# Row-wise softmax units from unit 6 on, earlier modulation weights, group loads one per pair, and P buffers given out by release, in a fused attention and gMLP block

## The chip, the cores and the metric

The kernel runs on one core of one Trainium2 chip. The metric is device time in microseconds (us). On one core there is no second die to compare with, so a run counts as fast when it lies within 1.5% of the fastest run of the same kernel. "Same": within 2%. Differences of a few us are given as ratios with a 95% interval, and the places where they arise are read from the traces.

## The reference

```python
mod = (_silu(c) @ w_mod).reshape(c.shape[0], 6, 1, -1)      # sa, ca, ga, sb, cb, gb: 512 each
h = _layernorm(x) * (1 + ca) + sa                           # x: 1 x 2048 x 512
x = x + ga * _A_ref(h, k_cache, v_cache, wq, wo)            # 32 heads, 8 K/V heads, 2048 keys, Dh 128
h = _layernorm(x) * (1 + cb) + sb
x = x + gb * _B_ref(h, w_in, w_sp, b_sp, w_out)             # gMLP with a 2048 x 2048 spatial matmul
```

Everything is bf16 in and out. `_A_ref` is plain softmax attention with four query heads to each K/V head. `ga` and `gb` are row vectors that scale the outputs of the two halves; the kernel needs them as rows repeated on all 128 partitions, `ga` first when the last K/V group's results are added, `gb` in the last matmul of the gMLP.

## The kernel before

Attention is cut into 128 units, `u = 16 * g + j`: one K/V group `g` (8 of them) and one tile `j` of 128 queries, with the group's four heads. Iteration `it` of the main loop holds unit `it`'s QK matmuls and exponentials, in 8 slots; into the same slots go the PV matmuls of an earlier unit, the output projection (Wo) of a still earlier one, and the Q projection of a later chunk. A unit comes in one of two forms.

* By columns: QK gives scores with keys on the partitions, ScalarE writes P already transposed (`pT`), PV takes 64 matmuls of 129 columns, and its small result `onorm` (128 x 512) goes through one DMA transpose to `oT`.
* By rows: QK gives scores with queries on the partitions, ScalarE writes P into four row buffers `pn` (three in the later home of `w_in`, called `win_sb`, one in `wmod_a`), VectorE scales it, and four DMA transposes of 128 x 2048, one per head, make `pT`. PV then takes 16 matmuls of 512 columns.

```python
TURN_A, TURN_B = 3 * CT, (HKV - 1) * NT            # 12, 112
def by_rows(u):
    return TURN_A <= u < TURN_B and u % 2 == 0
def pv_at(u):
    return u + 3 if by_rows(u) else u + 1
...
def turn_rows(u, hh):                              # two slots after the head's exponentials
    ...                                            # VectorE: sum, reciprocal, scale pn[hh]
    nc.sync.dma_start_transpose(out=pTs[u][:, :, hh * P : (hh + 1) * P], in_=pn[hh])
...
def mod_rows():                                    # ga and gb as rows
    mc_ps = bank("misc")
    for i, row in enumerate((0, 3)):
        mod_part(i, wmod_b, row * D, mc_ps)        # 16 matmuls of one column each
    for i, (part, rows) in enumerate(((2, ga_rows), (5, gb_rows))):
        cols = slice(part * NDT, (part + 1) * NDT)
        nc.vector.tensor_copy(out=modc[:, cols], in_=mc_ps[:, i * NDT : (i + 1) * NDT])
        line = dram.tile([D], FP32, name=f"mod{part}")
        nc.gpsimd.dma_start(out=line[:].rearrange("(dt p) -> p dt", p=P), in_=modc[:, cols])
        nc.gpsimd.dma_start(out=rows[:], in_=line[:].partition_broadcast(P))
...
at(2, 5, lambda: nc.gpsimd.dma_start(out=wmod_b, in_=wmod_dram[:, :, 2 * D : NMOD]))   # 2 MB
at(9, 4, mod_cols_b)
at(10, 4, mod_rows)
```

`at(it, slot, fn)` puts work into a slot. The last two lines of `mod_rows` are a round trip through DRAM: 512 floats are written, which turns a column layout into a line, and read back broadcast to all partitions. There are two such trips, one for `ga` and one for `gb`, both on GpSimd's queue, one behind the other. In this text they are called the trips.

## Time and profile before

| | before |
|---|---|
| median of three runs | 1317.13 us (1315.36 to 1318.52) |
| span of the profiled run, mean granted clock | 1314.1 us, 0.999 |
| row units | 50: units 12, 14, ... 110 |
| TensorE, ideal stream | 1293.1 us |
| TensorE, idle | 14.0 us |

The last two rows are worked out as in the prediction below, which also names the source of the time that a matmul is given: what a matmul takes over that time, from its start to the next one's, is counted as idle. It can be summed unit by unit.

The page's busy times and its DMA queues (packets, MB, share of 16 engines' time):

```profile
PE 1305.1 (99%) x9959; PEld 755.5 (57%) x9959; DVE 657.4 (50%) x1612; ACT 1105.0 (84%) x1461; POOL 52.0 (4%) x96
...
q1 hardware_dynamic: 530592, 135.97, 60.3%
```

The list of TensorE's waits (who waits, line, for whom: us in total, times, longest):

```profile
PE s_ps L1013 <- ACT wmod_a L1001: 1.6, 1, 1.6
PE o_ps L785 <- DVE onorm L767: 1.2, 1, 1.2
PE s_ps L1013 <- ACT pT L1020: 0.2, 1, 0.2
```

TensorE is busy 99% of the span, and no wait in the list is over 2 us. The first is the one late transpose of a row unit that the prediction finds at 541 us. GpSimd's timeline shows where the trips stood:

```profile
104.96 0.76 POOL L1173 DMA_DIRECT2D mod<-modc  x1 [42.79 <-DVE modc L1171]
113.98 0.56 POOL L1174 DMA_DIRECT2D ga_rows<-mod  x1 [8.27 <-DMA mod<-modc]
114.53 0.76 POOL L1173 DMA_DIRECT2D mod<-modc  x1
126.35 0.55 POOL L1174 DMA_DIRECT2D gb_rows<-mod  x1 [11.05 <-DMA mod<-modc]
```

The first trip was over before the first transposes of row unit 12 (121.4 us). Only the end of the second met them. The first two landed 8.5 and 11.2 us after their issue (the median of their form is 4.9), but TensorE did not wait for them. The loads of K/V group 2 were long done by then (59 to 61 us).

### The profile page before, as it was taken

To read this page: it belongs to the slowest core of one execution; us is meant where nothing else is said; L and a number is where in the kernel's file an instruction comes from. 1 tells how busy PE (TensorE), PEld (TensorE's weight loads), DVE (VectorE), ACT (ScalarE), POOL (GpSimd) and SP (SyncE) were. 2 spreads that over 40 slices of the span, in tenths; PEclk is the share of its full clock that TensorE was granted. 3 is DMA by queue.
4 is the path that set the end of the run, shared out by engine and by line. 5 is a ranking of instruction groups with operands and counts; after the bars stand their busy time and mean duration, and the time that the engine had idled before them with its cause. 6 is when DMAs were issued, how large, how long until landed. Compare 5 with 4: busy or idle time off the path is not lost.

```text
span 1314.1 us, 25092 instructions
## 1 busy us (share of the span) xinstructions
PE 1305.1 (99%) x9959; PEld 755.5 (57%) x9959; DVE 657.4 (50%) x1612; ACT 1105.0 (84%) x1461; POOL 52.0 (4%) x96
## 2 busy tenths in 40 slices
PE   9999999999999999999999999999999999999998
PEld 5666555555555555555555555555556666644445
DVE  6624445444454544444455544444452566784444
ACT  7899999999999999999999999999998899650000
POOL 1101000000000000000000000000000000120000
PEclk9999999999999999999999999999999999999999
DMA  7554988878988888988897877688762232143200
GB/s 181 123 67 58 180 161 141 140 125 158 153 144 138 144 141 138 135 142 157 153 143 129 155 141 144 124 166 151 140 126 76 45 62 48 29 117 80 69 21 27
DMA packets 537741, 156.79 MB, mean 119 GB/s; under 512 B 527280, under 2 KB 533680, under 8 KB 537616
## 3 DMA queue, kind: packets, MB, share of 16 engines
q1 hardware_dynamic: 530592, 135.97, 60.3%
q0 software_dynamic: 4432, 16.91, 4.6%
q10 hardware_dynamic: 2592, 2.23, 0.5%
q8 instruction: 80, 1.31, 0.4%
q14 instruction: 45, 0.37, 0.1%
HBM read 21.89 MB, written 2.10 MB: 18 GB/s over the span
## 4 chain that ended last, share of the span: by engine, by line
PE 98%; DMA 1%; DVE 0%; issue 0%; ACT 0%; ACTq 0%; DVEq 0%
PE o_ps L1069 21%; PE s_ps L1013 20%; PE o_ps L1048 13%; PE s_ps L994 13%; PE misc L1101 8%; PE misc L944 8%; PE misc L1426 7%; PE s_ps L1260 2%; PE s_ps L1299 2%; PE o_ps L1447 1%; DMA pT<-wmod_a 1%; PE o_ps L785 1%; PE s_ps L1447 1%; PE misc L854 0%; PE o_ps L944 0%; DVE hT L813 0%
## 5 line engine op out<-in xcount | busy, mean ns | idle before, releaser
L1020 ACT ACTIVATE wsp<-s_ps 128x1024 bf16<-128x1024 f32 x408 | 416.2, 1025 | 19.5 <-PE s_ps L1013 3.5
L1013 PE MATMUL s_ps<-qT,kT 128*128 128x512 bf16 x1248 | 370.9, 379 | 1.9 <-ACT wmod_a L1001 1.6
L1001 ACT ACTIVATE win_sb<-s_ps 128x1024 bf16<-128x1024 f32 x300 | 307.0, 1025 | 6.2 <-ACT win_sb L1001 0.8
L1069 PEld LDWEIGHTS <-wsp 128*128 128x128 bf16 x3264 | 218.5, 98 | 96.3
L1069 PE MATMUL o_ps<-v,wsp 128*128 128x129 bf16 x3264 | 251.6, 220 | 0.0
L994 PE MATMUL s_ps<-kT,qT 128*128 128x512 bf16 x800 | 237.9, 379 | 0.0
L1048 PE MATMUL o_ps<-pT,v 128*128 128x512 bf16 x800 | 237.3, 379 | 0.0
L1020 ACT ACTIVATE pT<-s_ps 128x1024 bf16<-128x1024 f32 x216 | 217.3, 1026 | 20.6 <-PE s_ps L1013 8.3
L1101 PE MATMUL misc<-wo_g,oT 128*128 128x512 bf16 x512 | 194.0, 379 | 0.0
L1013 PEld LDWEIGHTS <-kT 128*128 128x128 bf16 x1248 | 121.0, 98 | 117.0 <-issue 4.4
L944 PE MATMUL misc<-hT,wq_g 128*128 128x512 bf16 (+2 forms) x520 | 187.0, 371 | 0.1
L1069 PEld LDWEIGHTS <-pT 128*128 128x128 bf16 x1728 | 115.3, 98 | 49.6
L955 DVE CAST qT<-misc 128x512 bf16<-128x512 f32 x125 | 85.5, 684 | 112.2 <-PE misc L944 112.2
L1048 PEld LDWEIGHTS <-v 128*128 128x128 bf16 x800 | 78.2, 98 | 94.4
L1069 PE MATMUL o_ps<-v,pT 128*128 128x129 bf16 x1728 | 132.5, 220 | 0.0
L1057 DVE CAST oT<-o_ps 128x512 bf16<-128x512 f32 x50 | 34.6, 691 | 173.7 <-PE o_ps L1048 173.7
L1035 DVE TENSOR_SCALAR win_sb<-win_sb,rall 128x2048 bf16<-128x2048 bf16 x150 | 113.0, 753 | 5.7 <-DVE rall L1034 0.5
L994 PEld LDWEIGHTS <-qT 128*128 128x128 bf16 x800 | 78.2, 98 | 52.5 <-issue 0.2
L1001 ACT ACTIVATE wmod_a<-s_ps 128x1024 bf16<-128x1024 f32 x100 | 102.4, 1024 | 2.3 <-DMA pT<-wmod_a 2.3
L1426 PE MATMUL misc<-wsp,z 128*128 128x512 bf16 (+2 forms) x560 | 100.7, 336 | 0.0
L1080 DVE RECIPROCAL rall<-o_ps 128x2 f32<-128x2 f32 x156 | 26.6, 170 | 135.1 <-PE o_ps L1069 131.4
L1031 DVE TENSOR_TENSOR tot<-rs 128x1 f32<-128x1 f32 x200 | 30.7, 154 | 120.6 <-ACT win_sb L1001 119.1
(106 smaller groups left out, 856.5 us busy)
## 6 DMA issues: line engine op xcount, KB each, us to landing
wq_g<-in_A_wq_dram POOLq DMA_DIRECT2D x7, 512.0 KB, 5.5
v<-in_A_v_cache_dram POOLq DMA_DIRECT2D x7, 512.0 KB, 5.9
wo_g<-in_A_wo_dram POOLq DMA_DIRECT2D x7, 512.0 KB, 3.8
pT<-win_sb SPq DMA_TRANSPOSE x150, 4.9
wsp<-in_w_mod_dram POOLq DMA_DIRECT2D x1, 2048.0 KB, 10.4
out_dram<-yout ACTq DMA_DIRECT2D x16, 128.0 KB, 1.7
win_sb<-in_B_w_in_dram POOLq DMA_DIRECT2D x1, 1792.0 KB, 9.3
x_sb<-in_A_x_dram SPq DMA_DIRECT2D x3, 512.0 KB, 5.3
```

The costliest lines, as they stand in the source:

```text
L944: nc.tensor.matmul(ps[0][:, o0 : o0 + n], lhsT=wqs[g][:, dt, hh * DH : (hh + 1) * DH], rhs=hTs[ch][:, dt, c0 : c0 + n], start=(dt == 0), s ...
L955: nc.vector.tensor_copy(out=dst, in_=src)
L994: nc.tensor.matmul(s_ps[:, c * 512 : (c + 1) * 512], lhsT=qTs[b][:, hh, jj * P : (jj + 1) * P], rhs=groups[g]["kT"][:, k0 : k0 + 512], sta ...
L1001: nc.scalar.activation(out=pn[hh][:, half * HK : (half + 1) * HK], in_=s_ps[:], func=ACT.Exp, scale=inv_sqrt_dh, accum_out=rsums[u][:, i : ...
L1013: nc.tensor.matmul(s_ps[:, h * 512 : (h + 1) * 512].rearrange("p (r q) -> p r q", r=REP), lhsT=groups[g]["kT"][:, kt * P : (kt + 1) * P], ...
L1020: nc.scalar.activation(out=pTs[u][:, 2 * i : 2 * i + 2, :], in_=s_ps[:].rearrange("p (k q) -> p k q", k=2), func=ACT.Exp, scale=inv_sqrt_dh,)
L1035: nc.vector.tensor_scalar(out=pn[hh], in0=pn[hh], scalar1=rinv, scalar2=None, op0=ALU.mult)
L1048: nc.tensor.matmul(o_pss[u][:], lhsT=groups[g]["v1"][:, kt, 0:DH], rhs=pTs[u][:, kt, :], start=(kt == 0), stop=(kt == NKT - 1),)
L1057: nc.vector.tensor_copy(out=oTs[u][:], in_=o_pss[u][:].rearrange("p (r q) -> p r q", r=REP))
L1069: nc.tensor.matmul(o_ps[:, hh % 2, 0 : DH + 1], lhsT=pTs[u][:, kt, hh * P : (hh + 1) * P], rhs=groups[g]["v1"][:, kt, 0 : DH + 1], start=( ...
L1101: nc.tensor.matmul(X_ps[:], lhsT=oTs[u][:, hh, :], rhs=groups[g]["wo"][:, hh, :], start=(hh == 0), stop=(hh == REP - 1),)
L1426: nc.tensor.matmul(g_ps[:, :n], lhsT=z2[:, st, f * P : (f + 1) * P], rhs=wsp[t][:, st, c0 : c0 + n], start=(st == 0), stop=(st == NT - 1 a ...
```

## The change

Its intent: take more units in the form by rows, which costs TensorE a little less, by beginning with them at unit 6 rather than 12 and by adding units 112, 116 and 120; to have what they need in time, load the modulation weights earlier and compute their columns and rows in iterations 4 and 5 (the big buffer `wsp` that holds the weights then serves as a P buffer); spread each group's Wq, K, V and Wo loads over one load per pair of units; and give three P buffers out by whichever is released first.

```diff
-    TURN_A, TURN_B = 3 * CT, (HKV - 1) * NT
+    TURN_A, TURN_B = CT + 2, (HKV - 1) * NT
     def by_rows(u):
-        return TURN_A <= u < TURN_B and u % 2 == 0
+        return u % 2 == 0 if TURN_A <= u < TURN_B else u % 4 == 0 and TURN_B <= u < NU - CT
     def pv_at(u):
-        return u + 3 if by_rows(u) else u + 1
+        return u + 1 if not by_rows(u) else u + 3 if u < TURN_B else u + 5
+    users, homes = dict(pT0=-2, pT1=-1, wsp=TURN_A), {}
+    for u in range(NU):
+        homes[u] = min(users, key=lambda k: users[k])
+        assert users[homes[u]] < u
+        users[homes[u]] = pv_at(u)
...
-    at(2, 5, lambda: nc.gpsimd.dma_start(out=wmod_b, in_=wmod_dram[:, :, 2 * D : NMOD]))
-    at(TURN_B + 3, 5, lambda: nc.gpsimd.dma_start(out=win_sb, in_=win_dram))
-    at(9, 4, mod_cols_b)
-    at(10, 4, mod_rows)
+    at(2, 1, lambda: nc.gpsimd.dma_start(out=wmod_b, in_=wmod_dram[:, :, 2 * D : NMOD]))
+    at(NU - CT - 1, 2, lambda: nc.gpsimd.dma_start(out=win_sb, in_=win_dram))
+    at(4, 4, mod_cols_b)
+    at(5, 4, mod_rows)
...
-    at(TURN_B + 4, 0, wsp0)
+    at(NU + 1, 0, wsp0)
     for st in range(NT):
-        at(TURN_B + 4 + st // 2, 2 + 4 * (st % 2), lambda st=st: load_wsp(wsp[0], 0, st))
+        at(NU + 1 + st // 4, 2 * (st % 4), lambda st=st: load_wsp(wsp[0], 0, st))
     for g in range(1, HKV):
         it = (g - 1) * NT
-        at(it + 7, 6, lambda g=g: load_k(g))
-        at(it + 8, 3, lambda g=g: load_v(g))
-        at(it + 9, 3, lambda g=g: load_wo(g, nc.gpsimd))
-        at(it + 7, 3, lambda g=g: load_wq(g, nc.gpsimd))
+        at(it + 7, 4, lambda g=g: load_wq(g, nc.gpsimd))
+        at(it + 9, 5, lambda g=g: load_k(g))
+        at(it + 11, 4, lambda g=g: load_v(g))
+        at(it + 13, 4, lambda g=g: load_wo(g, nc.gpsimd))
```

Cut away here: the choice of tile in `qk`, the slots of the Q projection, and the lists of PV and Wo units in the main loop, which follow from the above.

More of the change, by code (lines that the diff above doesn't have):

```diff
@@ L982, in qk @@
         if i == 0:
-            if TURN_A <= u <= TURN_B + 1 and u % 2 == 1:
+            if homes[u] == "wsp":
                 pTs[u] = wspp.tile([P, NT, 512], BF16, name="wsp")
             else:
-                pTs[u] = late.tile([P, NKT, 512], BF16, name="pT")
+                pTs[u] = late.tile([P, NKT, 512], BF16, name=homes[u], bufs=1)
             if by_rows(u):
@@ L1230, in set_fill @@
             if hole:
-                it, slot = hole, k // 2
+                it, slot = divmod(hole * NSLOT + k // 2 - 1, NSLOT)
             if b == 1:
                 it, slot = 2 + (10 + k) // 16, (5 + k // 2) % 8
-            elif b == 2:
-                it, slot = (5, k // 2) if k < 8 else (it, slot)
             fill.setdefault((it, slot), []).append(fn)
@@ L1350 @@
             zs["z2"] = z2p.tile([P, NT, FH], BF16, name="z2")
-        pvs = [u for u in (it - 3, it - 1) if 0 <= u < NU and pv_at(u) == it]
-        wos = [u for u in (it - 5, it - 3) if 0 <= u < NU and pv_at(u) + 2 == it]
+        pvs = [u for u in (it - 5, it - 3, it - 1) if 0 <= u < NU and pv_at(u) == it]
+        wos = [u for u in (it - 7, it - 5, it - 3) if 0 <= u < NU and pv_at(u) + 2 == it]
         wf = [fn for u in wos for fn in wo_proj(u)]
```

## The prediction

> **What bounds the kernel now.** I read the page first, then the chain that ended last in order of time, then the timelines of single engines. The page's chain, by engine:
>
> ```profile
> PE 98%; DMA 1%; DVE 0%; issue 0%; ACT 0%; ACTq 0%; DVEq 0%
> ```
>
> TensorE is the bound almost everywhere, so the question is how dense its stream is. The same chain in order of time (start, length, piece) gives its rate:
>
> ```profile
> 72.35 0.45 PE o_ps L1069 x8
> ...
> 528.82 13.25 DMA pT<-wmod_a
> ...
> 1154.81 12.09 PE s_ps L1299 x56
> ```
>
> 56 matmuls of 512 columns in 12.09 us are 216 ns each; 8 of 129 columns in 0.45 us are 56 ns each. The DMA piece is the one large wait in the attention part: the fourth transpose of one row unit landed 13.25 us after its issue (the median of that form is 4.3), and PE lost 1.8 us (start-to-start distances of the matmuls, less 216 or 56 ns each).
>
> A unit by columns is 16 QK matmuls of 512, 64 PV matmuls of 129, and on average 4 of Wo and 4 of the Q projection: 24 x 0.2158 + 64 x 0.0563 = 8.78 us. A unit by rows replaces the 64 by 16 of 512: 40 x 0.2158 = 8.63 us. ScalarE's timeline shows both (start, length, instruction):
>
> ```profile
> 59.18 35.15 ACT L1020 ACTIVATE pT<-s_ps 128x1024 bf16<-128x1024 f32 x32 [0.29 <-PE s_ps L1013]
> ...
> 158.58 8.52 ACT L1020 ACTIVATE wsp<-s_ps 128x1024 bf16<-128x1024 f32 x8
> ...
> 176.02 8.52 ACT L1020 ACTIVATE wsp<-s_ps 128x1024 bf16<-128x1024 f32 x8
> ```
>
> Columns alone: (35.15 - 1.02)/31 x 8 = 8.81 us a unit. A pair of one row and one column unit: 176.02 - 158.58 = 17.44 us, which leaves 8.63 for the row unit. So turning a column unit into a row unit is worth only 0.17 us to PE. ScalarE is close behind: from 149.76 to 219.52 us, four pairs, it is busy 68.02 of 69.76 us.
>
> Subtracting the ideal stream from all of PE's start-to-start distances leaves 14.0 us of idle in the run: 5.1 in the first 20 us, 1.2 in units 12 to 15 (the turn to rows, bound by ScalarE), 1.8 at the late transpose, 1.9 in the MLP, the rest grains. This is all that a better schedule can win.
>
> **What the Trainium skill says.** "TensorE: Matmul & The Clock Gate", section "Back-to-back issue gap", gives an isolated gap of N/2.4 + 2.5 ns: 215.8 for 512 columns and 56.3 for 129. The trace agrees (216 and 56); the page's "sustained" figures of 81 and 131 ns are not what this stream shows. The same page, section "Architectural detail", says VectorE and GpSimd are strict FIFO; the trace agrees for GpSimd below. "Trainium Kernel Development and Optimization", section "Key Constraints", says that DMAs of the Sync, Scalar and GpSimd queues run on the same 16 engines and interleave; the next views show what that costs.
>
> **The change part by part.**
>
> *Row units.* Before, units 12, 14, ... 110: 50. After, 6, 8, ... 110 and 112, 116, 120: 56. Six more at 0.17 us: -1.0 us.
>
> *The turn.* In units 12 to 15 PE's work is 7.92 + 7.77 + 7.92 + 6.91 = 30.5 us (one PV is missing because a row unit's PV comes three units later, and the 16 Q matmuls fill in), but ScalarE needs 31.7 (first activation at 118.03, of unit 16 at 149.76). After, units 6 to 9 hold 8.35 + 7.34 + 8.78 + 7.77 = 32.2 us, because the projection for unit 12 on is no longer taken from them. Only the first pair (15.7 against some 16.1 for ScalarE) should wait: about 0.4 us instead of 1.2, so -0.8 us.
>
> *The last group.* A PV that was doubled up in iteration 113 is now doubled in 125; both are PE bound, 0. The first 16 W_sp transposes go from 1030-1098 us to after unit 127 (about 1139 us). One takes 1.26 us to issue and 2.6 to land, so 16 take some 20 us, and the spatial matmuls that read them start at 1184.9: hidden. Loading w_in after unit 120 (some 1075-1091 us, 9.3 us to land, needed at 1130.9): hidden.
>
> *"Loads one per pair".* GpSimd's timeline shows that placement in the program does not set when its loads go:
>
> ```profile
> 249.87 0.75 POOL L720 DMA_DIRECT2D wq_g<-in_A_wq_dram  x1 [64.68 <-PE misc L944]
> ...
> 528.90 0.75 POOL L720 DMA_DIRECT2D wq_g<-in_A_wq_dram  x1 [64.68 <-PE misc L944]
> ```
>
> The load issued at 249.87 (the third of this timeline after the first group's) stands in the program at iteration 39, about 353 us; GpSimd has nothing else to do, runs ahead and issues as soon as the last projection that reads the old buffer is over. Wq, V and Wo keep their order and their releasers, so in steady state they go when they did. The Wq load at 528.90 beside the transpose issued at 528.82 is the collision behind the 13.25 us; I see nothing that removes it. It was one of seven, so it may or may not recur: -0.5 us as an expectation.
>
> *The modulation weights (2 MB).* They move from iteration 2 slot 5 to slot 1, which puts them ahead of the next norm on GpSimd. The same FIFO makes this a large move:
>
> ```profile
> 21.77 1.05 POOL L681 TENSOR_TENSOR rstd_ln<-ve_ln,mhalf 128x4 f32<-128x4 f32 x1
> 35.77 0.23 POOL L677 TENSOR_SCALAR ve_ln<-mv 128x4 f32<-128x4 f32 x1 [12.95 <-DVE mv L697]
> 36.09 1.04 POOL L681 TENSOR_TENSOR rstd_ln<-ve_ln,mhalf 128x4 f32<-128x4 f32 x1
> 37.09 0.95 POOL L1218 DMA_DIRECT2D wsp<-in_w_mod_dram  x1
> ```
>
> Before, the load waited behind the norm at 36.09. After, nothing stands between 22.8 us and it. There it meets the four transposes of the first full chunk of h (Sync's queue), for which VectorE already waits:
>
> ```profile
> 23.30 5.90 SPq L844 DMA_TRANSPOSE hT<-xn  x4
> ...
> 38.10 8.01 SPq L844 DMA_TRANSPOSE hT<-xn  x4
> ```
>
> ```profile
> 30.57 1.38 DVE L813 TENSOR_SCALAR hT<-hT,modc 128x512 bf16<-128x512 bf16 x4 [3.02 <-DMA hT<-xn]
> ```
>
> ```profile
> 32.12 0.59 PE L944 MATMUL misc<-hT,wq_g 128*128 128x512 bf16 x2
> ```
>
> At 23.30 the transposes were alone: the fourth was issued at 27.26 and landed 3.2 us later, 7.2 us in all. At 38.10 they ran beside the 2 MB: fourth issued at 43.13, landed 6.0 later, 11.0 in all. If the 11.0 moves to the first chunk, it lands at 34.3, VectorE's first scaled piece is ready at some 34.7, and PE's first projection matmul, at 32.12 before, waits until about 35: +2.6 to +3.1 us, say +3.0, on the path because PE takes matmuls in order. I give this 0.8: +2.4. The columns and rows computed from these weights move from iterations 9 and 10 to 4 and 5 (45 and 53 us); the load, 10.4 us long, is there by 33.
>
> *Three buffers of P by release.* By hand, each unit finds a buffer whose PV is at least one iteration back: columns share one, rows alternate between two, and in the last group a row unit holds one for five iterations while columns use two. No new wait, 0.
>
> Sum: -1.0 - 0.8 - 0.5 + 2.4 = +0.1 us.
>
> **The rivals.**
> 1. *Only the gains come through.* If the 2 MB are slow enough to start, or the transposes win their share of the engines, the first chunk is not late: 1317.1 - 2.3 = 1314.8. For it: the load goes only half a microsecond ahead of the first transpose. Against: at 37.09 it was a full microsecond ahead and the transposes still took 3.8 us more.
> 2. *The row transposes become the limit.* In the pairs the 16 DMA engines are 0.86 busy and a row unit's fourth buffer is reused some 13 us after its transpose is issued; Wq, V and Wo of the second group, before at 59-61 us, now follow the modulation rows (two round trips through DRAM of 8 and 11 us) and go together at some 80-85 us, into the transposes of unit 8. A landing of 13 us just fits; one or two misses like the one at 541 cost 2 us each: 1319 to 1321. Against: 44 of 50 row units live beside such loads with one miss.
> 3. *ScalarE takes over.* A row unit adds 8 accumulator reads of 0.19 us, mostly under the activations. Alone, ScalarE passed units 12 to 15 at 15.9 us a pair against PE's 17.44, so six more row units leave it behind PE: no change.
>
> **Range and chances.** Gains total at most 2 to 4 us and the one loss I see is 3, with another 2 to 4 possible: 1313 to 1320. The three runs of before alone span 3.2 us. Since the single collision is the only thing against the change and I may have overrated it, I set the point a little below the sum, at 1316.4. Two per cent is 26 us, twice all the idle time that PE has; nothing in the change moves that much, so 0.98 for within.
>
> **What would show it.** Right: 56 row units at 8.63 us; pairs at 17.44 from unit 10; VectorE's wait before the first scaling of h up from 3.02 to about 7 us and PE idle for some 3 us near 32; the modulation load issued near 22.8; Wq at unchanged times in steady state; PE idle in the turn under 0.6 us. Wrong: no PE idle near 32 (rival 1), new PE waits on transposes of P (rival 2), or a pair longer than 17.5 us (rival 3). A W_sp transpose that ends PE's wait near 1185 us would break the last-group step.

## The result, and the profile after

| | before | after |
|---|---|---|
| median | 1317.82 us (1315.36 to 1318.52, 4 runs) | 1331.49 us (1327.86 to 1334.19, 4 runs) |
| span of the profiled run, clock | 1314.1 us, 0.999 | 1329.4 us, 0.995 |
| TensorE, ideal stream | 1293.1 us | 1292.2 us |
| TensorE, idle | 14.0 us | 30.2 us |

The ratio is 1.0105, 95% interval 1.0077 to 1.0133: "same" by the 2% rule, but slower beyond doubt, and outside the predicted range of 1313 to 1320. Ratios here are the mean time of one kernel's fast runs over that of the other's fast runs of the same rounds, so not quite the ratio of the medians quoted. The medians here are of four runs of each kernel; the experiments bring their own runs of before.

The spans differ by 15.3 us: 16.2 us more idle, less 0.9 us of shorter stream. The page after, busy times, then the Sync and ScalarE DMA queue, then the chain that ended last:

```profile
PE 1307.2 (98%) x9671; PEld 744.3 (56%) x9671; DVE 679.9 (51%) x1666; ACT 1109.9 (83%) x1509; POOL 53.3 (4%) x96
...
q1 hardware_dynamic: 577248, 147.77, 66.1%
...
PE 96%; DMA 3%; DVE 0%; ACT 0%; issue 0%; SPq 0%; ACTq 0%; DVEq 0%
```

Two points of the chain have gone from TensorE to DMA. The queue carries 11.8 MB more. That is what six more row units cost it: four transposes of 128 x 2048 bf16 are 2.10 MB, one of 128 x 512 is 0.13 MB, and 6 x 1.97 = 11.8. TensorE's waits after:

```profile
PE s_ps L1020 <- ACT wmod_a L1008: 7.5, 2, 7.3
PE misc L1108 <- DMA oT<-onorm: 3.9, 1, 3.9
PE misc L944 <- DVE hT L813: 2.9, 1, 2.9
```

The last of these is the predicted one. The 2 MB load was issued at 22.64 us, VectorE waited 7.16 us for the transposed h, and the projection matmul came at 35.03 us; before, it came at 32.12. VectorE's line, then TensorE's:

```profile
34.57 1.38 DVE L813 TENSOR_SCALAR hT<-hT,modc 128x512 bf16<-128x512 bf16 x4 [7.16 <-DMA hT<-xn]
```

```profile
35.03 0.70 PE L944 MATMUL misc<-hT,wq_g 128*128 128x512 bf16 x2 [2.89 <-DVE hT L813]
```

The other two waits are new, and both are in unit 8. The stretch from 82 us to 115 us, by engine (stretch, us; busy us of PE, PEld, DVE, ACT, POOL with the number of instructions; granted clock; DMA share; GB/s):

```profile
82.00:104.50 22.50, 11.23 (x92) 6.88 (x91) 7.46 (x17) 9.00 (x17) 3.43 (x5) 0.87 1.02 163
104.50:115.00 10.50, 10.50 (x41) 4.30 (x41) 2.18 (x5) 8.51 (x10) 0.00 (x0) 0.80 1.14 182
```

In the first 22.5 us TensorE and ScalarE are both busy half of the time or less, while packets stand on the DMA engines all the time (the share adds up what the packets took, waiting included). The waits run one after another. TensorE waits some 4 us at 87.8 for the transpose `oT` of unit 5, whose source was ready at 75.25 but which stood behind a stretched transpose of P on Sync until 84.52; and 7.5 us at 97 for ScalarE, which itself waits for the fourth transpose of unit 6's P to be over before it may overwrite the row buffer `wmod_a`. Both idles also cost clock: it reads 0.5 from 91.7 to 95.1 us and from 101.9 to 108.8 us. Ten matmuls of 512 columns between 104.50 and 108.72 take 4.22 us instead of 10 x 0.216 = 2.16, so 2.1 us more are lost there, and 1.5 us after the first idle. The Trainium skill, page "TensorE: Matmul & The Clock Gate", section "What's actually happening", says that the clock falls to half after an idle window of about 3.4 us and comes back after a busy one of the same length. Here the falls came 3.7 and 4.8 us after the idles began (88.0 and 97.2), and the clock came back 3.2 and 4.3 us after they ended; these two agree, but the last section has one that does not.

What were the transposes doing? Sync's timeline, then GpSimd's, then the piece of the chain:

```profile
69.92 14.49 SPq L1045 DMA_TRANSPOSE pT<-win_sb  x3
84.52 1.21 SPq L1096 DMA_TRANSPOSE oT<-onorm  x1
85.83 7.20 SPq L1045 DMA_TRANSPOSE pT<-wmod_a  x1
```

```profile
62.88 0.83 POOL L1180 DMA_DIRECT2D mod<-modc  x1
72.34 0.57 POOL L1181 DMA_DIRECT2D ga_rows<-mod  x1 [8.63 <-DMA mod<-modc]
72.90 0.76 POOL L1180 DMA_DIRECT2D mod<-modc  x1
84.39 0.55 POOL L1181 DMA_DIRECT2D gb_rows<-mod  x1 [10.73 <-DMA mod<-modc]
84.93 0.76 POOL L720 DMA_DIRECT2D wq_g<-in_A_wq_dram  x1
...
86.97 0.85 POOL L738 DMA_DIRECT2D wo_g<-in_A_wo_dram  x1
```

```profile
85.83 17.41 DMA pT<-wmod_a
```

The first three transposes of row unit 6 were issued in the time when the two trips stood in flight. The third was issued at 77.88 and Sync was held in it until 84.42; the second trip's write (2 KB) was issued at 72.90 and released GpSimd at 84.39. Then Sync went on at once, and GpSimd, released at the same moment, issued three loads of 512 KB in 2.9 us. The fourth transpose, behind all this, was issued at 85.83 and landed after 17.41 us; the median of that form was 4.3 us before.

The rate at which the DMA engines moved data from 62 to 90 us (40 slices of 0.7 us) shows what these transposes met:

```profile
GB/s 23 0 0 45 145 86 101 114 73 135 19 16 11 61 115 236 68 0 147 290 284 210 236 291 8 0 0 0 0 4 216 118 287 269 3 0 82 152 108 183
```

Two of the low stretches, near 70 us and from 79 to 82.7 us, end shortly before GpSimd is released from a trip's write (72.34 and 84.39). In the second not one packet starts or ends, while 24 stand in flight. So the engines did not run short of bandwidth there: they stood still.

The "loads one per pair" did not happen: three of the loads of the second group went together. GpSimd runs ahead of the program and was held only by the trips.

Idle, by place, after: 3.3 us in unit 2 (the late h), 1.5 in units 4 and 5 (the one-column matmuls, which moved here from iterations 9 and 10), 0.9, 0.1, 13.2 and 2.2 in units 6, 7, 8 and 9, 0.35 at unit 44, 1.9 after the attention, some 5 at the start, and small remainders elsewhere. Units 6 to 9 together: 16.4 us, against 1.2 us that the turn cost before (in units 12 to 15). The steady state is as predicted. ScalarE's timeline, two successive column units:

```profile
228.58 8.52 ACT L1027 ACTIVATE pT<-s_ps 128x1024 bf16<-128x1024 f32 x8
...
246.02 8.52 ACT L1027 ACTIVATE pT<-s_ps 128x1024 bf16<-128x1024 f32 x8
```

A pair takes 246.02 - 228.58 = 17.44 us, the same as before.

### The profile page after: what moved, and what is told of

It reads as the page before. It is cut to its first block, busy times and chain, and to the rows that moved or that the text cites. A ratio compares the mean times of both kernels' runs of the same rounds, so it can differ in the third digit from the quotient of the medians.

```text
span 1329.4 us, 24732 instructions
## 1 busy us (share of the span) xinstructions
PE 1307.2 (98%) x9671; PEld 744.3 (56%) x9671; DVE 679.9 (51%) x1666; ACT 1109.9 (83%) x1509; POOL 53.3 (4%) x96
## 4 chain that ended last, share of the span: by engine, by line
PE 96%; DMA 3%; DVE 0%; ACT 0%; issue 0%; SPq 0%; ACTq 0%; DVEq 0%
PE o_ps L1076 19%; PE s_ps L1020 18%; PE o_ps L1055 14%; PE s_ps L1001 14%; PE misc L1108 8%; PE misc L944 8%; PE misc L1431 7%; DMA pT<-wmod_a 2%; PE s_ps L1265 2%; PE s_ps L1304 2%; PE o_ps L1452 1%; PE o_ps L785 1%; PE s_ps L1452 1%; DMA hT<-xn 0%; ACT win_sb L1008 0%
## 5 line engine op out<-in xcount | busy, mean ns | idle before, releaser
L1027 ACT ACTIVATE pT<-s_ps 128x1024 bf16<-128x1024 f32 x560 | 568.8, 1024 | 36.4 <-PE s_ps L1020 12.9
L1076 PEld LDWEIGHTS <-pT 128*128 128x128 bf16 x4480 | 300.1, 98 | 131.8 <-issue 1.0
L1008 ACT ACTIVATE win_sb<-s_ps 128x1024 bf16<-128x1024 f32 x336 | 343.6, 1023 | 12.2 <-PE s_ps L1001 5.4
L1076 PE MATMUL o_ps<-v,pT 128*128 128x129 bf16 x4480 | 345.1, 220 | 0.0
L1001 PE MATMUL s_ps<-kT,qT 128*128 128x512 bf16 x896 | 267.2, 380 | 0.4 <-ACT win_sb L1008 0.4
L1055 PE MATMUL o_ps<-pT,v 128*128 128x512 bf16 x448 | 134.2, 381 | 0.0
L1055 PE MATMUL o_ps<-wsp,v 128*128 128x512 bf16 x448 | 132.6, 379 | 0.0
L1001 PEld LDWEIGHTS <-qT 128*128 128x128 bf16 x896 | 87.8, 98 | 59.8 <-issue 1.4
L1431 PEld LDWEIGHTS <-z 128*128 128x128 bf16 x560 | 50.6, 98 | 48.4
L1121 DVE TENSOR_TENSOR xacc<-misc,xacc 128x512 f32<-128x512 f32 x112 | 76.2, 680 | 0.0
L944 PEld LDWEIGHTS <-wq_g 128*128 128x128 bf16 x528 | 50.7, 98 | 32.1 <-issue 3.9
```

What stands on the lines that cost most here:

```text
L944: nc.tensor.matmul(ps[0][:, o0 : o0 + n], lhsT=wqs[g][:, dt, hh * DH : (hh + 1) * DH], rhs=hTs[ch][:, dt, c0 : c0 + n], start=(dt == 0), s ...
L1001: nc.tensor.matmul(s_ps[:, c * 512 : (c + 1) * 512], lhsT=qTs[b][:, hh, jj * P : (jj + 1) * P], rhs=groups[g]["kT"][:, k0 : k0 + 512], sta ...
L1008: nc.scalar.activation(out=pn[hh][:, half * HK : (half + 1) * HK], in_=s_ps[:], func=ACT.Exp, scale=inv_sqrt_dh, accum_out=rsums[u][:, i : ...
L1027: nc.scalar.activation(out=pTs[u][:, 2 * i : 2 * i + 2, :], in_=s_ps[:].rearrange("p (k q) -> p k q", k=2), func=ACT.Exp, scale=inv_sqrt_dh,)
L1055: nc.tensor.matmul(o_pss[u][:], lhsT=groups[g]["v1"][:, kt, 0:DH], rhs=pTs[u][:, kt, :], start=(kt == 0), stop=(kt == NKT - 1),)
L1076: nc.tensor.matmul(o_ps[:, hh % 2, 0 : DH + 1], lhsT=pTs[u][:, kt, hh * P : (hh + 1) * P], rhs=groups[g]["v1"][:, kt, 0 : DH + 1], start=( ...
```

## The experiments

The question is what made the 16.4 us in units 6 to 9. Three candidates stand side by side at 62 to 88 us: the trips in flight beside row transposes; the group's loads in a bunch right after them; and the row units themselves, begun so early that too much must happen at once. Beside this, the 2 MB load (3 us) and the rearranged tail are to be tested. Twelve kernels ran, all correct. Each was timed in the same rounds as the kernel before; "ratio" is always to the kernel before.

### The 2 MB load, put back, and moved alone

In the changed kernel, the load goes back behind the norm; in the kernel before, it alone is moved ahead.

```diff
 (in the changed kernel)
-    at(2, 1, lambda: nc.gpsimd.dma_start(out=wmod_b, ...))
+    at(2, 5, lambda: nc.gpsimd.dma_start(out=wmod_b, ...))
 (in the kernel before)
-    at(2, 5, lambda: nc.gpsimd.dma_start(out=wmod_b, ...))
+    at(2, 1, lambda: nc.gpsimd.dma_start(out=wmod_b, ...))
```

> The changed kernel with one line put back: the 2 MB of modulation weights in iteration 2 slot 5, behind the norm on GpSimd. In the changed kernel PE waits 3.1 us at 31.9 us for the first scaled chunk of h, and VectorE 7.2 us. Theory (the 2 MB beside the four transposes of h cause it): PE's wait near 32 us vanishes, VectorE's wait is back to 3 us, the kernel is 3 us faster than the changed one, about 1328 us, and the 13 us lost in unit 8 stay as they are, 3 us earlier. Rival (the wait has another cause, for instance the new order of work on VectorE): it stays at 3 us. A side effect to look for: the load lands at some 47 us, just before its first reader at 49 us.

> The kernel before with one line changed: the 2 MB of modulation weights moved ahead of the norm (iteration 2 slot 1), nothing else. Theory (the load beside the transposes of h): PE waits 3 us near 32 us, the kernel is 3 us slower than before, about 1320.5 us. Rival (the wait in the changed kernel comes from another part): no wait there, within 1 us of before.

Put back: 1328.98 us, ratio 1.0073 (1.0047 to 1.0099). Moved alone in the kernel before: 1323.12 us, ratio 1.0037 (1.0011 to 1.0063). VectorE's wait for h, first with the load put back, then with the load moved alone:

```profile
31.68 1.38 DVE L813 TENSOR_SCALAR hT<-hT,modc 128x512 bf16<-128x512 bf16 x4 [3.94 <-DMA hT<-xn]
```

```profile
34.70 1.38 DVE L813 TENSOR_SCALAR hT<-hT,modc 128x512 bf16<-128x512 bf16 x4 [7.18 <-DMA hT<-xn]
```

The wait follows the load, both ways. In time: 0.0032 x 1318 = 4.2 us for putting it back, the difference of two ratios that are each uncertain by some 3.5 us, so this time alone shows little and the waits show more; 0.0037 x 1318 = 4.9 us for moving it alone, uncertain by 3.4. TensorE's own wait was 3.1 us at 32.0 us when it was moved alone, and unit 2 lost 4.65 us there in all, because the clock read 0.5 for 3.4 us after it. This kernel also lost 4.2 us in units 12 to 15 (before: 1.2), where its second trip was still in flight; no run tests that part alone. In the kernel with the load put back, units 8 and 9 still lost 9.9 and 2.6 us. So this part of the prediction stands, and it is not the main loss. That kernel also lost 5.9 us after the attention, discussed with the tail.

### The trips moved out of the row units' way

In the changed kernel, the matmuls of `mod_rows` stay, but the trips wait until iteration 113, shortly before `ga` is needed.

```diff
+    def mod_trips():
+        for part, rows in ((2, ga_rows), (5, gb_rows)):
+            ...                                     # VectorE copies the columns to held
+            nc.gpsimd.dma_start(out=line[:].rearrange("(dt p) -> p dt", p=P), in_=held[:])
+            nc.gpsimd.dma_start(out=rows[:], in_=line[:].partition_broadcast(P))
...
+    at(TURN_B + 1, 4, mod_trips)
```

> The changed kernel with only the two round trips of the modulation rows through DRAM moved, from iteration 5 to iteration 113 (held there by a copy on VectorE). GpSimd is then free at 63 us, and Wq, V and Wo of the second group go at 63 to 66 us instead of 85 to 88. Theory A (the trips, and the loads that they hold back into unit 8, make the loss there): PE's idle in units 8 and 9 falls from 15.3 us (13.2 + 2.2) to under 2, the kernel is 13 to 15 us faster than the changed one, about 1317 us. Theory B (the DMA engines are simply too busy from unit 6 on, wherever the loads go): the loads now meet the transposes of h and of unit 6, and more than 5 us of idle stay between 60 and 110 us, about 1322 to 1326 us.

It took 1320.3 us, ratio 1.0009 (0.9985 to 1.0033). With GpSimd free, the loads of the second group went at 64.6 to 67 us. The same stretch as above:

```profile
67.50:102.50 35.00, 35.00 (x268) 20.16 (x266) 19.79 (x49) 34.16 (x52) 0.14 (x1) 1.00 1.14 187
```

TensorE is busy throughout, with the same row units. Over the same stretch of time the changed kernel has a DMA share of 1.20 at 133 GB/s, against 1.14 at 187 here: its packets took longer and moved less. Units 6 to 9 lost 0.5 us (unit 6 alone 0.3, the figure that a later expectation quotes). The rows themselves are therefore not too early for the DMA engines. Not all came back in time: the second trip, now in flight from 1015.4 to 1028.8 us beside row unit 116, cost 2.3 us there, unit 2 lost 4.7 us and the part after the attention 3.5. This kernel takes away the trips and the bunching at once, so the next ones separate the two.

### The loads spaced, the trips left

Before each of the three loads GpSimd reads a value that row unit 6, 10 or 12 writes; so the loads can no longer bunch, and the trips stay where they were.

```diff
+    def pace(u):
+        t = stat.tile([P, 1], FP32, name="pace")
+        c = u * REP + REP - 1
+        nc.gpsimd.tensor_scalar(out=t[:], in0=rall[:, c : c + 1], scalar1=LN_EPS, ...)
+    for u in (6, 10, 12):
+        at(u + 1, 4, lambda u=u: pace(u))
```

> The changed kernel with the loads of the second group really one per pair: GpSimd reads a sum of row unit 6, 10 and 12 before Wq, V and Wo. The two trips stay at iteration 5. If the bunch of three loads (1.5 MB at 85 to 88 us) made the transpose of unit 8 take 17.4 us: the wait of 7.5 us and the slow clock after it (2.2 us) vanish, while the wait of 4.1 us for the transposed output of unit 5 stays, since its transpose was issued at 84.5 us, before any load: 9 to 10 us faster than the changed kernel, about 1321.5 us. If the trips alone are at fault, 0 to 2 us faster. If the row transposes alone overload the engines, no change.

It took 1322.32 us, ratio 1.0022 (1.0000 to 1.0044). TensorE's waits:

```profile
PE misc L1108 <- DMA oT<-onorm: 4.1, 1, 4.1
PE misc L944 <- DVE hT L813: 2.8, 1, 2.8
```

The 4.1 us wait for `oT` stays and the 7.5 us wait is gone. The clock still fell behind the first (a mean of 0.63 between 92 and 96 us, 0.94 in the next 4 us). Units 6 to 9 lost 6.8 us instead of 16.4. In the changed kernel, then, the bunch of loads adds some 10 us to what the trips do.

### Row units from 12 again, all else as changed

```diff
-    TURN_A, TURN_B = CT + 2, (HKV - 1) * NT
+    TURN_A, TURN_B = 3 * CT, (HKV - 1) * NT
```

> The changed kernel with the turn to rows back at unit 12 (one constant); the early load, the early trips, the loads, the rows in the last group and the late W_sp loads stay. Trips (63 to 84 us) and bunched loads (85 to 88 us) then meet no transpose of P. Theory (the loss in units 8 and 9 needs the row transposes there): those 15.3 us vanish, while the 3 to 4.7 us near 32 us and the 1.2 us of the turn at 12 to 15 stay: some 12 us faster than the changed kernel, about 1.004 of before. Rival (PE itself starves there through the loads): a stall of several us stays between 85 and 105 us.

It took 1319.02 us, ratio 1.0009 (0.9990 to 1.0027). GpSimd's timeline shows the trips and the bunch of loads in the old place:

```profile
64.90 0.83 POOL L1180 DMA_DIRECT2D mod<-modc  x1
...
87.35 0.55 POOL L1181 DMA_DIRECT2D gb_rows<-mod  x1 [11.55 <-DMA mod<-modc]
87.89 0.76 POOL L720 DMA_DIRECT2D wq_g<-in_A_wq_dram  x1
```

Units 6 to 9, now by columns, lost 0.1 us. The trips and the loads cost TensorE nothing by themselves: they need row transposes beside them. A transpose `oT` issued at 78.01 us, with the second write in flight, landed after 9.2 us here too (median of its form before: 2.5), but nothing waited for it. The kernel came out some 4 us faster than I expected, which the interval just excludes; the 3.3 us in unit 2 stayed as expected.

### The loads ahead of the trips

If the bunch right behind the trips were a necessary part, then loads that go before the trips should leave only the trips' share.

```diff
-        at(it + 7, 4, lambda g=g: load_wq(g, nc.gpsimd))
+        at(5 if g == 1 else it + 7, 3 if g == 1 else 4, lambda g=g: load_wq(g, nc.gpsimd))
 (V and Wo of the second group likewise, ahead of mod_rows)
```

> The changed kernel with Wq, V and Wo of the second group issued in iteration 5, before the two trips through DRAM, so that they go near 63 us while the trips stay in the first row units (65 to 87 us). With the run that only paced the loads (PE wait of 4.3 us for the transposed output stayed, 7.5 us and the slow clock went) and the one that moved trips and loads (both went) this separates the two causes. Theory (trips make the 4 us wait, bunched loads the 7.5): a wait of 3 to 5 us near 87 us stays, none of 7 us near 97, 9 to 11 us faster than the changed kernel, about 1.0025 of before. Rival (the loads make both, the trips only delay them): no wait over 1 us in units 6 to 9, about 1.001 of before.

It took 1329.55 us, ratio 1.0102 (1.0067 to 1.0136): my expectation of a ratio near that of the spaced loads was wrong. The loads went at 64.3 to 67.4 us, and the trips, pushed behind them, took longer and lay deeper in the row units. GpSimd's timeline, then TensorE's waits:

```profile
67.36 0.76 POOL L1180 DMA_DIRECT2D mod<-modc  x1
...
94.55 0.55 POOL L1181 DMA_DIRECT2D gb_rows<-mod  x1 [11.66 <-DMA mod<-modc]
```

```profile
PE s_ps L1001 <- ACT win_sb L1008: 5.9, 1, 5.9
```

Units 6 to 9 lost 11.1 us with no load behind the trips; loads at this place without the trips had left 0.5 us. So the trips beside the row transposes are sufficient for a loss of that size, and a bunch of loads behind them is an aggravation, not a condition. How much they cost depends on which transposes they meet: 6.8 us in the kernel with spaced loads, 11.1 here.

### The writes alone beside the row transposes

A trip is a write to DRAM in 4-byte pieces and a broadcast read. Here the loads go early, both writes are issued in iteration 7 and the reads wait until iteration 113.

```diff
 (on top of the kernel with the loads ahead)
+    at(TURN_A + 1, 5, mod_writes)      # both 2 KB writes
+    at(TURN_B + 1, 4, mod_reads)       # both broadcast reads
```

> My last expectation fell: with the loads ahead of the trips the loss stayed (1.0102), so the trips beside row transposes are enough. A trip is a write of 2 KB in pieces of 4 bytes to DRAM and a read of it broadcast to 128 partitions (256 KB). Here both writes go in iteration 7 (near 82 us, held there by a copy on VectorE), both reads in iteration 113, and Wq, V and Wo near 64 us; everything else as changed. The run with both trips at 113 and the loads at 65 to 67 us had PE idle of 0.3 us in units 6 to 9. Theory (the writes hold up the transposes of P while they are in flight): Sync's transposes between 82 and 95 us take 5 us or more to issue and PE waits 3 to 9 us in units 8 to 10: 1.003 to 1.008 of before. Rival (the broadcast reads do it): under 1 us of idle there, about 1.002 of before.

It took 1326.85 us, ratio 1.0100 (1.0073 to 1.0127). GpSimd's two writes, Sync's transpose just behind them, ScalarE's wait for it, and TensorE's wait:

```profile
80.12 1.50 POOL L1188 DMA_DIRECT2D mod<-held  x2 [14.30 <-DVE held L1186]
```

```profile
85.61 5.04 SPq L1045 DMA_TRANSPOSE pT<-wmod_a  x1
```

```profile
88.58 1.02 ACT L1008 ACTIVATE win_sb<-s_ps 128x1024 bf16<-128x1024 f32 x1 [3.74 <-DMA pT<-win_sb]
```

```profile
PE s_ps L1001 <- ACT win_sb L1008: 3.4, 1, 3.4
```

With the writes as the only addition to the row units, the same picture returns: transposes held on Sync, ScalarE waiting for a row buffer, TensorE waiting 3.4 us behind it. The size of the wait was as expected. In this trace 172 matmul records are missing (23 of QK), so the sum of idle can't be made from them, but ScalarE's timeline gives its size. From its first activation of unit 6 to that of unit 10 it took 39.3 us (66.34 to 105.62), and 32.9 us in the kernel with both trips at 113 (68.15 to 101.02), where 0.5 us of that was idle: by this estimate units 6 to 9 lost some 6.9 us. From 85 to 88 us the DMA engines moved only 14 GB/s. The total time was above what I expected: the profile is of the fastest of the four runs (1323.68 us), and the slowest (1331.47 us) has no trace, so the rest stays open.

### No trips at all: the rows made by TensorE

The rows can be had without DRAM. The left operand of a matmul is `silu(c)` for one k, repeated over 128 columns; the product with the weights is then the wanted row on all 128 partitions. Eight matmuls of 512 columns replace 32 of one column and both trips. The 2 MB load goes back behind the norm as well.

```diff
     def mod_rows():
-        ...                                         # 32 one-column matmuls, two trips
+        r_ps = [bank("misc"), bank("o_ps")]
+        for kt in range(NDT):
+            lhs = res.tile([P, P], BF16, name="sc_bc", bufs=2)
+            nc.vector.tensor_scalar(out=lhs[:], in0=ones_bf[:], scalar1=sc[:, kt : kt + 1],
+                                    scalar2=None, op0=ALU.mult)
+            for i, row in enumerate((0, 3)):
+                nc.tensor.matmul(r_ps[i][:], lhsT=lhs[:], rhs=wmod_b[:, kt, row * D : (row + 1) * D],
+                                 start=(kt == 0), stop=(kt == NDT - 1))
+        for i, rows in enumerate((ga_rows, gb_rows)):
+            nc.vector.tensor_copy(out=rows[:], in_=r_ps[i][:])
...
-    at(5, 4, mod_rows)
+    at(7, 3, mod_rows)
```

Three kernels have this early part and differ in the tail: exactly as changed; with the last group as before; and with an attempt of mine to mend the tail, in which the W_sp transposes are queued behind the last transpose of the second norm.

```diff
 (attempt at the tail)
-        at(NU + 1 + st // 4, 2 * (st % 4), lambda st=st: load_wsp(wsp[0], 0, st))
+        at(NU + 3 + (st + 5) // NSLOT, (st + 5) % NSLOT, lambda st=st: load_wsp(wsp[0], 0, st))
```

> The changed kernel with the two early repairs (2 MB behind the norm, rows on TensorE without the trips through DRAM) and its tail exactly as changed: row units 112, 116, 120, W_sp transposes after unit 127 mixed with the last transposes of the second norm. The fully mended kernel lost 9 us at 1231 us by my own repair of the tail; the kernel with the last group as before ran at 0.9978 of before. Theory (the late part costs PE 0 to 4 us at the start of the spatial matmuls and gains 0.5): PE's idle after the attention is 1.9 to 6 us, no wait of 9 us at 1231, time 0 to 4 us above the kernel with the last group as before: 0.998 to 1.001 of before. Rival (the wait of 9 us came from the late part itself, not from my repair): it is there again, 1.005.

> As the fully mended kernel, but with the last group as in the kernel before (no row units there, W_sp and w_in early). It has three row units fewer: 0.5 us more of ideal stream than the fully mended one, and no risk in the tail. Theory: within 1 us of the fully mended kernel, 0.998 to 1.000 of before. If the mended tail still loses, this one is faster by that loss.

> The changed kernel with three repairs: the 2 MB behind the norm again; the two modulation rows made on TensorE by 8 matmuls of 512 columns against a broadcast vector in iteration 7 (no trip through DRAM, so GpSimd is free at 63 us and the loads go before the row transposes); the first 16 W_sp transposes queued behind the last transposes of the second norm. If the three mechanisms are the whole of the loss, PE has no wait over 1 us after the start: ideal stream 1293 us, idle 12 to 13 us, span 1312 to 1314, 0.997 to 0.9995 of before. If they are not, a wait stays that I have not named.

Tail as changed: 1315.9 us, ratio 0.9964 (0.9945 to 0.9984). Last group as before: 1316.19 us, ratio 0.9978 (0.9965 to 0.9992). Both are faster than both given kernels, by a little ("same" by the 2% rule, but the intervals exclude 1). I had expected the first of them to be the slower one; the two intervals overlap. Units 6 to 9 lost 1.7 us in each, most of it one wait of about 1 us for the left operand from VectorE. Against the changed kernel this is 0.0141 x 1318 = 18.6 us by the ratios. Against the kernel before, the gain of 3 to 5 us is more than one profile of each shows: idle plus stream was 15.4 + 1293.9 us and 12.0 + 1294.3 us, against 14.0 + 1293.1. Single profiles differ by a few us as the runs do, and I leave the exact split of that gain open.

My attempt at the tail was a miss: 1325.97 us, ratio 1.0059 (1.0045 to 1.0073). TensorE's new wait, and VectorE's under it:

```profile
PE misc L1438 <- DVE gb L1453: 8.7, 1, 8.7
```

```profile
DVE yout L1472 <- DMA out_dram<-yout: 15.9, 2, 15.2
```

An output tile was ready at 1214.30 us, but its DMA was issued only at 1235.72. The trace shows its issuer waiting on a semaphore whose last user was one of the delayed W_sp transposes, issued at 1232.89 and landed at 1235.64. In this program the DMAs of Sync and ScalarE take turns at eight completion semaphores. I infer from this that the output DMA could not start before an unrelated one of the other engine was over; no run tests it alone.

### No trips in the kernel before

Is the missing trip worth something by itself?

```diff
 (in the kernel before)
-    at(10, 4, mod_rows)
+    at(10, 4, lambda: mod_row(0, ga_rows))      # the same matmuls, one row at a time
+    at(11, 4, lambda: mod_row(3, gb_rows))
```

> The kernel before with one thing changed: the two modulation rows made on TensorE in iterations 10 and 11, no trips through DRAM. This asks what of the gain of the mended early part (0.9978 of before, PE idle 12.0 us against 14.0) is due to the turn at unit 6 and what to the missing trips. If the trips alone matter: 0.997 to 0.999 of before, as good as the mended early part. If the earlier turn is the gain: 0.999 to 1.001, since the rows cost PE some 1 us more and the trips of before overlap little with row transposes.

It took 1319.28 us, ratio 0.9997 (0.9978 to 1.0016). So the missing trips alone show no gain, as expected for the case that the earlier turn is the gain. But making the rows cost TensorE 2.8 us of idle in units 10 and 11 (two waits of about 1.3 us for the left operand) and 1.6 us of longer stream here, so a gain of that order can have been hidden, and what the repaired kernels owe to the turn stays open.

### The last group as before

The changed kernel with only its tail undone: no row units after 110, `w_in` and the W_sp transposes early again.

```diff
     def by_rows(u):
-        return u % 2 == 0 if TURN_A <= u < TURN_B else u % 4 == 0 and TURN_B <= u < NU - CT
+        return TURN_A <= u < TURN_B and u % 2 == 0
...
-        at(NU + 1 + st // 4, 2 * (st % 4), lambda st=st: load_wsp(wsp[0], 0, st))
+        at(TURN_B + 4 + st // 2, 2 + 4 * (st % 2), lambda st=st: load_wsp(wsp[0], 0, st))
```

> The changed kernel with the last group as before: columns only from unit 112 on, w_in and the first 16 W_sp transposes loaded where they were. Theory (W_sp transposes queued after unit 127 on Sync hold up the last transposes of the second norm, so VectorE waits 2.5 to 7 us for them, against 1.1 before, and PE 0 to 4 us at the start of the spatial matmuls): VectorE's wait is back near 1 us and PE's idle after the attention back at 1.9 us (1.9 to 5.9 in the runs so far); the loss in units 8 and 9 stays whole. Time: three rows fewer cost 0.5, the tail gives 0 to 4: 0 to 3 us faster than the changed kernel. Rival (the tail's wait comes from elsewhere, say the doubled PV in iteration 125): the wait stays.

It took 1332.04 us, ratio 1.0103 (1.0087 to 1.0118), the changed kernel's time again. The tail is worth nothing, in either direction, to within the some 4 us by which the difference of the two ratios is uncertain. VectorE's wait for the last transposed norm, first in the changed kernel, then here:

```profile
DVE hT L1152 <- DMA xnT<-xn: 2.5, 1, 2.5
```

```profile
DVE hT L1154 <- DMA xnT<-xn: 1.2, 1, 1.2
```

Moving the W_sp transposes does lengthen this wait: 1.2 becomes 2.5 us. In the changed kernel TensorE lost the same 1.9 us after the attention as the kernel before; in the kernel with the load put back the wait was 7.1 us and TensorE lost 5.9; with the rows by TensorE it was 4.8 and TensorE lost 2.2. So the tail has a small and variable cost that lies mostly beside other work.

### Summary of the runs

| kernel | ratio to before | idle in units 6 to 9 |
|---|---|---|
| changed kernel | 1.0105 | 16.4 us |
| loads ahead of the trips | 1.0102 | 11.1 us |
| writes alone beside row units | 1.0100 | some 6.9 us (estimate from ScalarE) |
| loads spaced, trips as changed | 1.0022 | 6.8 us |
| trips at iteration 113 | 1.0009 | 0.5 us |
| row units from 12 | 1.0009 | 0.1 us |
| no trips, last group as before | 0.9978 | 1.7 us |
| no trips, tail as changed | 0.9964 | 1.7 us |

## Why the prediction was wrong, and where it was right

The sum was +0.1 us; the profile shows +15.3.

*Row units, -1.0 us: right.* There are 56, and the ideal stream went from 1293.1 to 1292.2 (0.15 us for each of the six, as 8.78 less 8.63 gives, rather than 0.17). Pairs take 17.44 us.

*The turn, -0.8 us: wrong, and this is the step that failed.* The first pair did wait, 0.9 us in unit 6 against the predicted 0.4. But the turn as a whole went from 1.2 us to 16.4, so the term should have been +15.2. The prediction worked it out from TensorE's and ScalarE's work alone and then let the two things that now surround the turn cost nothing: it said of the columns and rows only that they "move from iterations 9 and 10 to 4 and 5", and it counted the loads as moved too. It did see the meeting. Rival 2 places the trips and then the loads "at some 80-85 us, into the transposes of unit 8"; they went at 84.9 to 87.8. Its sizing failed: "A landing of 13 us just fits; one or two misses ... cost 2 us each". The landing was 17.41 us, the transpose `oT` on the same queue waited as well (4.1 us of TensorE), and the two idles cost 3.6 us of clock. What the rival set against this, that "44 of 50 row units live beside such loads with one miss", is not in the trace: 23 of the 50 have a DMA of GpSimd in flight beside their transposes, and the steady loads go one at a time (249.9, 306.6 and 323.9 us for one group), never three together. And its cause was half right: it looked at the loads, while the experiments show that the trips in flight beside row transposes are enough (11.1 us with no load behind them; some 6.9 us with the two writes alone), need row units beside them (0.1 us with rows from 12 on), and are made worse by the bunch of loads (16.4 against 6.8 us when spaced).

A clue was in the trace before. The prediction gives the trips as 8 and 11 us, and did not ask why 2 KB should take that long. The page "DMA: Bandwidth & Descriptors" of the Trainium skill, section "Anatomy of one DMA — SWDGE (gpsimd) path", gives about 2.0 us as the fixed cost of a DMA, most of it the wait for the write's receipt, and longest where the target is HBM. Against that, a GpSimd wait of 8.27 to 11.05 us suggests that these 512 pieces of 4 bytes are a special case, and it was a reason to ask whether what shares the engines with them would wait too: the kernel before already had two slow transposes and a standstill there (124.0 to 125.6 us).

*The late transpose, -0.5 us: right in sign, by luck.* The wait of 1.8 us did not recur, and another of 0.35 us came at unit 44; such waits came back in some of the experiments (3.1 us in two waits in the fastest kernel), so it is chance rather than gain.

*The modulation weights, +3.0 us at 0.8: right.* 3.3 us in unit 2, VectorE's wait at 7.16 us where about 7 was predicted, the projection at 35.03 where 35 was. Two experiments, one each way, confirm the cause. The load was moved past the norm by GpSimd's order alone, which is what the prediction read from its timeline.

*The last group, 0 us: right for the time, not quite for the reason.* It was called hidden; VectorE's wait grew by some 1.4 us, TensorE's loss did not.

*Three buffers, 0 us: right.* No wait in the list is for a P buffer; the waits are for the row buffers `win_sb` and `wmod_a`, which the change did not touch.

What is not settled is the mechanism inside the DMA engines: why a 2 KB write in 4-byte pieces takes 8 to 14 us, and why transposes issued meanwhile are held up. The write's own packets are short: in the kernel before, the first write is 16 packets of 128 bytes, over by 106.7 us, 1.7 us after its issue, and GpSimd was released only at 113.98. In the changed kernel packets of those transposes stand for up to 4.4 us, and an instruction fetch at 78 us for 4.3, while the second write is outstanding. I looked through all fourteen traces for standstills of this kind, over 1.2 us long with more than ten packets in flight. Seven traces have one with a trip's write not yet landed (1.6 to 3.8 us): before, changed, the 2 MB load put back and moved alone, loads spaced, loads ahead, and last group as before. The one with spaced loads has another, of 1.5 us, while the broadcast read is in flight. None is in the four kernels without trips, in the one with row units from 12, or in the one with both trips at 113. With the writes alone beside row units there is none either, only the low rate of 14 GB/s given above. So the standstill goes with trips beside row transposes; this does not say why. An experiment with the same bytes in one contiguous piece would have told whether the pieces matter; it was not run.

## What to carry to other kernels

When work is moved, ask not only what it costs and whether it is in time, but what else will be in flight beside it: here a 2 KB round trip through DRAM that cost nothing among column units cost over 10 us among row units, whose transposes share the engines. A queue that runs ahead of its program sends loads when their buffers come free, so an obstacle in it turns loads that were spaced in the source into a bunch behind it; the timeline of the issuing engine shows this, the source does not. And a small transfer with a long landing in the trace before is a warning: replace it by work on the bound engine if that is cheap enough (eight matmuls here), and the rest of the change may turn out to be sound.

## What the Trainium skill lacked or had wrong

* "DMA: Bandwidth & Descriptors", section "Anatomy of one DMA — SWDGE (gpsimd) path", gives about 2.0 us of fixed cost. A 2 KB write to DRAM in 4-byte pieces held GpSimd for 8.27 to 13.47 us here. The page does advise against such patterns; what it lacks is their time, and that other DMAs can stand still meanwhile (no packet from 79.0 to 82.7 us).
* The same page, section "Rules for kernel authors", says that a transpose next to ordinary DMAs needs nothing. That is said of correctness, and the runs agree; what the page lacks is the time. Beside such writes and the loads behind them one transpose stood 17.41 us from issue to landing (median 4.3), and Sync was held 7.20 us in one issue.
* No page says that DMAs of Sync and ScalarE that take turns at the same completion semaphores can delay one another, as I infer from one trace: an output tile ready at 1214.30 us went at 1235.72, behind an unrelated transpose.
* "TensorE: Matmul & The Clock Gate", section "Back-to-back issue gap": its isolated figures agree (216 and 56 ns); its sustained ones of 131 and 81 ns do not describe this stream, which is sustained for over a millisecond at 216 and 56. Its section "What's actually happening" has the clock fall after an idle window of some 3.4 us. Shorter idles were enough here: in the kernel with the 2 MB load moved alone TensorE was idle from 32.25 to 35.16 us, and the clock read 0.5 from 34.8 to 38.2; in the changed kernel an idle of 2.9 us at the same place left it at 1.
